# A one-core attention and MLP kernel on Trainium2: five tile pools entered in another order, three small tiles moved

## The chip, the cores and the metric

The kernel runs on one core of a Trainium2 chip. The metric is device time in microseconds (us) of one execution; 1 us is 1000 ns. The core has a matrix engine (PE, with its weight loads shown apart as PEld), a vector engine (DVE), a scalar engine (ACT), a general engine (POOL) and a queue engine that issues most transfers (SP). Operands lie in the on-chip memory SBUF, 128 partitions wide; a tile has the same start address in each partition. Matrix products are written to PSUM.

## The reference

Local attention with a window of 32 and a few global tokens, and then an MLP with gelu, all in float32:

```python
B, H, Sl, D = 8, 8, 512, 64; Sg = 32; window = 32
s_g = scale * q_g @ concat(k_g, k_l).T;  out_g = softmax(s_g) @ concat(v_g, v_l)
s_ll = where(|i - j| <= window, scale * q_l @ k_l.T, -1e9);  s_lg = scale * q_l @ k_g.T
out_l = softmax(concat(s_lg, s_ll)) @ concat(v_g, v_l)
x = concat(out_g, out_l) as (4352, 512)       # 8 * (32 + 512) tokens, 8 heads * 64
h = x @ w_in                                  # 512 -> 2048
g = 0.5 * h * (1 + erf(h / sqrt 2))
out = g @ w_out                               # 2048 -> 512
```

## The kernel before

The tokens are cut into 17 chunks of 256: two halves for each of the 8 batches, and one chunk "g" that gathers the global tokens of all batches. Attention makes a chunk of x in the tile `xs`, head pair by head pair, while the MLP of an earlier chunk runs; a planner with costs and due times, written out at the top of the file, fixes the order of the steps on each engine. PE is shared by both, and its MLP products stand between those of attention.

From the second chunk on, the MLP splits each float32 operand into a high part that float32r holds (`xh`, `gh`, `wh`) and the rest (`xl`, `gl`, `wl`), and adds three products for each one. A product has a stationary operand (`lhsT`), which an LDWEIGHTS loads into the array, and a moving operand (`rhs`), which streams through it:

```python
hi, lo = (w[2 * f][:, c * P:c * P + P] for w in (wh, wl_))          # ml_hc
nc.tensor.matmul(out=h, lhsT=hi, rhs=xh, ...)                       # L709
nc.tensor.matmul(out=h, lhsT=hi, rhs=xl, ...)                       # L710
nc.tensor.matmul(out=h, lhsT=lo, rhs=xh, ...)                       # L711
...
hi, lo = wh[2 * f + 1], wl_[2 * f + 1]                              # ml_o
nc.tensor.matmul(out=acc[t], lhsT=gh[:, f % 2, tsl], rhs=hi, ...)   # L744
nc.tensor.matmul(out=acc[t], lhsT=gl[:, f % 2, tsl], rhs=hi, ...)   # L745
nc.tensor.matmul(out=acc[t], lhsT=gh[:, f % 2, tsl], rhs=lo, ...)   # L746
```

So in the first half of the MLP (lines L709 to L711, tile `h`, 256 columns) the weights are loaded and x streams, and in the second (L744 to L746, tile `acc`, 512 columns) gelu's parts are loaded and the weights stream. For each of 16 values of f a chunk has 12 products of the first kind (three for each of four c) and 6 of the second (three for each of two t). Over 16 chunks that makes 3072 and 1536. The first chunk uses whole float32 products instead (L705, tiles `xf` and `wf`, and L736, tiles `wf` and `gf`).

ACT makes `gf` from `h` (L279), ACT or DVE rounds it to `gh` (L132, L134), POOL subtracts to `gl` (L139). The same helpers make `xh` and `xl` from `xs`. Of attention's products this text uses two: L517 (`o` from `vs`, stationary, and `at`, moving, 256 columns) and L563 (`sg`, the global scores: `gs` is stationary, `k` moving, 288 columns in the first half of a batch and 256 in the second). The two tiles of each `k` part take turns, by whether the head pair is even or odd. L650 (`go` from `agt`, stationary, and `vgs`, moving) serves the global tokens.

SBUF tiles come from pools, and a pool's place follows from the order in which the pools are entered and the sizes of the ones ahead. `cp`, `ap`, `sm`, `gp`, `xp`, `wp` and `wr` are entered in this order; `gp` holds gelu's parts, `xp` holds `xh` and `xl`, `wp` holds `wl` (and `wf`), `wr` holds `wh`, `sm` small columns of the softmax.

Of the kernel before, what the change touches and what calls it, by code (L numbers as in the profile page):

```python
# [8 lines left out]
F32 = mybir.dt.float32  # L9
F32R = mybir.dt.float32r  # L10
BF16 = mybir.dt.bfloat16
# [9 lines left out]
WS, WF = 192, 224  # L21
# [63 lines left out]
def attn_mlp(ctx, tc, q_l, k_l, v_l, q_g, k_g, v_g, w_in, w_out, out):  # L85
# [5 lines left out]
    P = 128  # L91
# [6 lines left out]

    cp = ctx.enter_context(tc.tile_pool(name="cp", bufs=1))
    ap_ = ctx.enter_context(tc.tile_pool(name="ap", bufs=1))  # L100
    sm = ctx.enter_context(tc.tile_pool(name="sm", bufs=4))


    gp = ctx.enter_context(tc.tile_pool(name="gp", bufs=2))
    xp = ctx.enter_context(tc.tile_pool(name="xp", bufs=1))
    ps_s = ctx.enter_context(tc.tile_pool(name="ps_s", bufs=2, space=PSUM))
    ps_t = ctx.enter_context(tc.tile_pool(name="ps_t", bufs=2, space=PSUM))
    ps_h = ctx.enter_context(tc.tile_pool(name="ps_h", bufs=2, space=PSUM))
# [5 lines left out]

    masks = []
    for half in range(2):
        m = cp.tile([P, WF], BF16, name=f"mask{half}")
        nc.gpsimd.memset(m, 0.0)
        for c0, k0, w in (((0, -32, 32), (64, 0, 160)) if half == 0 else ((0, -32, 160), (192, 128, 32))):
            v = m[:, c0:c0 + w]  # L120
            nc.gpsimd.affine_select(out=v, in_=v, pattern=[[-1, w]], base=32 - k0,
                                    channel_multiplier=1, compare_op=ALU.is_ge, fill=-BIG)
            nc.gpsimd.affine_select(out=v, in_=v, pattern=[[1, w]], base=32 + k0,
                                    channel_multiplier=-1, compare_op=ALU.is_ge, fill=-BIG)
        masks.append(m)
# [453 lines left out]
    KG = (0, 160, 288, 416)  # L579

    def gu_min(e, g):
        t = sm.tile([P, 3], F32, name="gsm", tag="gsm", bufs=2)
        st[g, "mn"], st[g, "sum"], st[g, "ri"] = t[:, 0:1], t[:, 1:2], t[:, 2:3]
        mn = st[g, "mn"]
        nc.vector.tensor_reduce(out=mn, in_=sgr[g[1]], axis=AX.X, op=ALU.max)
        nc.vector.tensor_scalar_mul(out=mn, in0=mn, scalar1=-SC)
# [183 lines left out]
    bufs = {"s": 2, "t": 2, "h": 2, "gh": 2, "gl": 2, "sm": 4, "wr": NF}  # L770
# [24 lines left out]
    for n, u in enumerate(units):  # L795
        b, half, p = u
# [209 lines left out]
    def starts(x, k):  # L1006
        t = x["at"][k]
        n = {}
        for kind, y in x["takes"]:
            n[kind] = n.get(kind, 0) + 1  # L1010
        for kind, m in n.items():
            h = sorted((freed.get(y, 1e9) for y in taken.get(kind, [])), reverse=True)
            i = bufs.get(kind, 1) - m
            if i < len(h):
                if h[i] == 1e9:
                    return None
                t = max(t, h[i] + LAT0)
        if k == "a" and x["size"]:
            t = max(t, dma - 1.5)
        return t  # L1020
# [4 lines left out]
    while any(ready.values()):  # L1025
        can = []
        for k in ENG:
            for x in ready[k]:
                t = starts(x, k)
                if t is None:  # L1030
                    continue
                t = max(t, busy[k])
                if k == "p" or k == "v" and x["port"]:
                    t = max(t, port)
# [11 lines left out]
        t, due, _, x, k = best  # L1046
# [86 lines left out]
```

## Time and profile before

| | |
|---|---|
| median of 3 runs | 1050.46 us (1049.86 to 1051.32) |
| the profiled execution | 1050.12 us, of which the span from its first to its last instruction is 1048.3 us |
| PE busy | 1016.1 us, 97% of the span |
| PEld busy | 903.3 us, 86% |
| DVE, ACT, POOL busy | 680.4, 676.9, 380.4 us (65%, 65%, 36%) |
| granted PE clock | 1.00 |

In the groups of instructions a row gives line, engine, operation, tiles (written from read), shape and count, then the busy time in us and the mean duration of one in ns. PE works on several products at a time, so a product's duration is longer than the time from its start to the next one's start. This text calls the latter the pitch; it is read from start times.

### The profile page before, as it was taken

The numbers are of one execution on the slowest core, as the hardware profiler recorded it, in microseconds if no ns is written. First come the engines' busy times: TensorE is split into PE (matmuls) and PEld (weight loads), VectorE is DVE, ScalarE is ACT, GpSimd is POOL, SyncE is SP. The second block draws the span as 40 slices with busy tenths as digits, with TensorE's granted clock in tenths as the row PEclk, the third lists the DMA queues.
The fourth block names the chain that finished last, engine by engine and source line by source line (L and its number), as shares of the span: only waits on it lengthen the run. The fifth ranks groups of instructions, "written<-read, shape, count | busy, mean of one in ns | idle before, by whom it ended". The sixth has DMA issues, their size and how long they took to land.

```text
span 1048.3 us, 21420 instructions
## 1 busy us (share of the span) xinstructions
PE 1016.1 (97%) x7000; PEld 903.3 (86%) x7000; DVE 680.4 (65%) x2089; ACT 676.9 (65%) x1617; POOL 380.4 (36%) x427
## 2 busy tenths in 40 slices
PE   4989999999999999999999999999999999999998
PEld 2756699998988989998999999998999989999897
DVE  2978968667676768677775777577676777561000
ACT  2978886776667766777575666577565766573221
POOL 2111575243332534334342525244333434243121
PEclk9999999999999999999999999999999999999999
DMA  7785332214221233213322332213322332101000
GB/s 186 226 256 201 55 77 45 53 43 81 49 64 30 42 84 65 59 36 60 82 39 56 61 71 59 61 34 76 64 42 51 64 72 59 44 14 56 1 21 21
DMA packets 277983, 72.29 MB, mean 69 GB/s; under 512 B 263152, under 2 KB 271344, under 8 KB 277872
## 3 DMA queue, kind: packets, MB, share of 16 engines
q1 hardware_dynamic: 271792, 68.57, 28.5%
q10 hardware_dynamic: 6080, 2.36, 0.9%
q8 instruction: 55, 0.90, 0.3%
q14 instruction: 56, 0.46, 0.2%
HBM read 61.41 MB, written 9.44 MB: 68 GB/s over the span
## 4 chain that ended last, share of the span: by engine, by line
PE 84%; DMA 4%; ACT 4%; DVE 3%; SPq 3%; issue 1%; POOL 0%; ACTq 0%; DVEq 0%; POOLq 0%
PE h L709 11%; PE h L711 10%; PE h L710 10%; PE acc L744 10%; PE acc L745 10%; PE acc L746 10%; PE o L517 5%; PE s L406 4%; PE t L480 2%; PE acc L736 2%; PE h L705 2%; PE go L650 2%; ACT a_t L279 1%; PE sg L563 1%; DMA wraw<-in_moe_w_in_dram 1%
## 5 line engine op out<-in xcount | busy, mean ns | idle before, releaser
L139 POOL TENSOR_TENSOR gl<-gf,gh 128x512 fp32r<-128x512 f32 x127 | 167.9, 1322 | 406.4 <-ACT gh L132 282.1
L709 PE MATMUL h<-xh,wh 128*128 128x256 f32 x1024 | 299.1, 292 | 1.4 <-ACT gf L279 1.4
L711 PE MATMUL h<-xh,wl 128*128 128x256 f32 x1024 | 289.7, 283 | 0.0
L710 PE MATMUL h<-xl,wh 128*128 128x256 f32 x1024 | 289.3, 283 | 0.0
L744 PE MATMUL acc<-wh,gh 128*128 128x512 f32 x512 | 206.3, 403 | 0.0
L709 PEld LDWEIGHTS h<-xh,wh 128*128 128x128 f32 x1024 | 195.0, 190 | 10.4 <-ACT gf L279 1.8
L745 PE MATMUL acc<-wh,gl 128*128 128x512 f32 x512 | 201.7, 394 | 0.0
L746 PE MATMUL acc<-wl,gh 128*128 128x512 f32 x512 | 200.6, 392 | 0.0
L710 PEld LDWEIGHTS h<-xl,wh 128*128 128x128 f32 x1024 | 195.2, 191 | 5.7 <-issue 0.7
L711 PEld LDWEIGHTS h<-xh,wl 128*128 128x128 f32 x1024 | 195.0, 190 | 0.0
L279 ACT ACTIVATE gf<-h 128x512 f32<-128x512 f32 x136 | 81.1, 597 | 73.2 <-POOL gl L139 37.7
L279 ACT ACTIVATE a_t<-a_t,sm 128x192 f32<-128x192 f32 (+1 forms) x256 | 116.9, 458 | 2.9 <-DVE sm L431 2.0
L746 PEld LDWEIGHTS acc<-wl,gh 128*128 128x128 f32 x512 | 96.4, 188 | 21.6
L425 DVE CUSTOM_DVE_ANT_0 a_t<-s,mask 128x192 f32<-128x192 f32 (+1 forms) x256 | 80.4, 367 | 48.0 <-PE s L406 48.0
L132 ACT ACTIVATE gh<-gf 128x512 fp32r<-128x512 f32 x95 | 60.0, 632 | 77.2 <-PE acc L746 76.1
L744 PEld LDWEIGHTS acc<-wh,gh 128*128 128x128 f32 x512 | 96.9, 189 | 13.0
L745 PEld LDWEIGHTS acc<-wh,gl 128*128 128x128 f32 x512 | 97.0, 189 | 11.3
L500 DVE TENSOR_TENSOR at<-t,at 128x512 fp32r<-128x512 f32 (+1 forms) x112 | 67.7, 618 | 38.7 <-ACT at L132 38.2
L132 ACT ACTIVATE at<-t 128x512 fp32r<-128x512 f32 (+1 forms) x112 | 59.4, 541 | 49.8 <-PE t L481 25.9
L139 POOL TENSOR_TENSOR vs<-vr,vs 128x512 fp32r<-128x512 f32 x56 | 74.8, 1336 | 42.6 <-DVE vs L134 23.9
L279 ACT ACT_TABLE_LOAD x69 | 88.5, 1283 | 1.2
L548 DVE TENSOR_TENSOR xs<-o,xs 64x256 f32<-64x256 f32 x112 | 46.1, 412 | 51.9 <-ACT xs L543 50.6
(132 smaller groups left out, 1730.9 us busy)
## 6 DMA issues: line engine op xcount, KB each, us to landing
wraw<-in_moe_w_out_dram SPq DMA_DIRECT2D x16, 512.0 KB, 7.6
raws<-in_v_l_dram SPq DMA_DIRECT2D x64, 128.0 KB, 2.5
out_dram<-ob SPq DMA_DIRECT2D x32, 256.0 KB, 2.1
raws<-in_k_l_dram SPq DMA_DIRECT2D x224, 36.0 KB, 1.9
vr<-in_v_l_dram SPq DMA_DIRECT2D x113, 64.0 KB, 2.2
wraw<-in_moe_w_in_dram SPq DMA_DIRECT2D x14, 512.0 KB, 7.4
raws<-in_q_l_dram SPq DMA_DIRECT2D x224, 32.0 KB, 1.8
raws<-in_v_g_dram SPq DMA_DIRECT2D x128, 16.0 KB, 1.9
```

The source lines that it names most:

```text
L132: nc.scalar.activation(out=out, in_=in_, func=AF.Copy)
L139: (nc.vector if e == "v" else nc.gpsimd).tensor_sub(**kw)
L279: nc.scalar.activation(func=func, **kw)
L425: nc.vector.tensor_tensor_reduce(out=a_t[:, j, aoff[half][i]:aoff[half][i] + w], in0=s[:, c:c + w], in1=masks[half][i], scale=1.0, scalar= ...
L500: nc.vector.tensor_sub(out=at[:, 1], in0=st.pop((u, "t", j))[:, :n * P].rearrange("p (n q) -> p n q", q=P), in1=at.bitcast(F32)[:, 0])
L517: nc.tensor.matmul(out=o[:, :, qsl], lhsT=l.rearrange("p s e -> p (s e)"), rhs=r, start=(n == 0), stop=(n == 3), skip_group_check=True)
L709: nc.tensor.matmul(out=h, lhsT=hi, rhs=xh, start=(c == 0 and not (key == (0, 0) and f < HQ and f % 2)), stop=False, skip_group_check=True)
L710: nc.tensor.matmul(out=h, lhsT=hi, rhs=xl, start=False, stop=False, skip_group_check=True)
L711: nc.tensor.matmul(out=h, lhsT=lo, rhs=xh, start=False, stop=(c == NCC - 1), skip_group_check=True)
L744: nc.tensor.matmul(out=acc[t], lhsT=gh[:, f % 2, tsl], rhs=hi, start=(f == 0), stop=False)
L745: nc.tensor.matmul(out=acc[t], lhsT=gl[:, f % 2, tsl], rhs=hi, start=False, stop=False)
L746: nc.tensor.matmul(out=acc[t], lhsT=gh[:, f % 2, tsl], rhs=lo, start=False, stop=(f == NF - 1))
```

## The change

`sm` is entered behind `gp` and not ahead of it. One of the two masks moves from `cp` into a new pool `mp`, entered behind `sm`, and the two `gsm` tiles move from `sm` into a new pool `sg`, entered behind `xp`.

```diff
     cp = ctx.enter_context(tc.tile_pool(name="cp", bufs=1))
     ap_ = ctx.enter_context(tc.tile_pool(name="ap", bufs=1))
+    gp = ctx.enter_context(tc.tile_pool(name="gp", bufs=2))
     sm = ctx.enter_context(tc.tile_pool(name="sm", bufs=4))
-    gp = ctx.enter_context(tc.tile_pool(name="gp", bufs=2))
+    mp = ctx.enter_context(tc.tile_pool(name="mp", bufs=1))
     xp = ctx.enter_context(tc.tile_pool(name="xp", bufs=1))
+    sg = ctx.enter_context(tc.tile_pool(name="sg", bufs=2))
...
-        m = cp.tile([P, WF], BF16, name=f"mask{half}")
+        m = (cp if half else mp).tile([P, WF], BF16, name=f"mask{half}")
...
-        t = sm.tile([P, 3], F32, name="gsm", tag="gsm", bufs=2)
+        t = sg.tile([P, 3], F32, name="gsm", tag="gsm")
```

A mask takes 448 bytes of a partition, the four `sm` tiles 4 x 64, the two `gsm` tiles 2 x 32. So all of `cp` behind the mask and all of `ap` start 448 bytes lower, `gp` 448 + 256 + 64 = 768 bytes lower, `xp` 64 bytes lower, and the weights' pools where they were. The order of the instructions on every engine, their shapes and their waits are those of before; only addresses differ. Start addresses of the tiles modulo 512 bytes (each f, c and t step inside a tile is a multiple of 512 bytes):

| tile | before | after |
|---|---|---|
| `xh`, `xl`, `xf` | 448 | 384 |
| `gf`, `gh`, `gl` | 448 | 192 |
| `wh`, `wl`, `wf` | 448 | 448 |
| `agt`, `vgs` (L650) | 448 | 448 |
| `at`, moving in L517 / `vs`, stationary | 128 / 384 | 192 / 448 |
| `gs`, stationary in L563 | 256 | 320 |
| `k` read by L563, 256 columns, even / odd pair | 256 / 0 | 320 / 64 |
| `xs` | 256 | 320 |

## The prediction

> **What bounds the kernel now.** I read the page from the top: busy time and granted clock, then the chain that ended last, then the groups.
>
> ```profile
> PE 1016.1 (97%) x7000; PEld 903.3 (86%) x7000; DVE 680.4 (65%) x2089; ACT 676.9 (65%) x1617; POOL 380.4 (36%) x427
> PEclk9999999999999999999999999999999999999999
> PE 84%; DMA 4%; ACT 4%; DVE 3%; SPq 3%; issue 1%; POOL 0%; ACTq 0%; DVEq 0%; POOLq 0%
> PE h L709 11%; PE h L711 10%; PE h L710 10%; PE acc L744 10%; PE acc L745 10%; PE acc L746 10%; PE o L517 5%; PE s L406 4%; PE t L480 2%; PE acc L736 2%; PE h L705 2%; PE go L650 2%; ACT a_t L279 1%; PE sg L563 1%; DMA wraw<-in_moe_w_in_dram 1%
> L709 PE MATMUL h<-xh,wh 128*128 128x256 f32 x1024 | 299.1, 292 | 1.4 <-ACT gf L279 1.4
> L711 PE MATMUL h<-xh,wl 128*128 128x256 f32 x1024 | 289.7, 283 | 0.0
> L710 PE MATMUL h<-xl,wh 128*128 128x256 f32 x1024 | 289.3, 283 | 0.0
> L744 PE MATMUL acc<-wh,gh 128*128 128x512 f32 x512 | 206.3, 403 | 0.0
> L745 PE MATMUL acc<-wh,gl 128*128 128x512 f32 x512 | 201.7, 394 | 0.0
> L746 PE MATMUL acc<-wl,gh 128*128 128x512 f32 x512 | 200.6, 392 | 0.0
> ```
>
> PE is busy all through at the full granted clock, and the six MLP lines alone hold 11+10+10+10+10+10 = 61% of the chain, 639 us. The other engines are busy two thirds of the time or less. So the time is a count of products times their pitch, and a nanosecond on each MLP product is about 4.6 us on PE (3072 + 1536 of them). How long a product holds PE, and how its successor's load runs beside it, is in the order of time, first near the end, where attention no longer stands between, then in the middle:
>
> ```profile
> 1000.25 0.28 PE L709 MATMUL h<-xh,wh 128*128 128x256 f32 x1
> 1001.69 0.40 PE L744 MATMUL acc<-wh,gh 128*128 128x512 f32 x1
> 1003.08 0.28 PE L709 MATMUL h<-xh,wh 128*128 128x256 f32 x1
> ```
>
> ```profile
> 600.05 0.28 PE L710 MATMUL h<-xl,wh 128*128 128x256 f32 x1
> 600.06 0.19 PEld L711 LDWEIGHTS h<-xh,wl 128*128 128x128 f32 x1
> ```
>
> Between the first two starts lie 12 products of 256 columns: 1.44 us / 12 = 120 ns each. Between the second and the third lie 6 of 512 columns: 1.39 / 6 = 232 ns each. Together 3072 x 0.120 + 1536 x 0.232 = 725 us of pitch, of which the chain's 639 us are 88%. The other pair shows the load for the next product (L711) starting 0.01 us after the running product (L710): one reads its moving tile while the other reads the next stationary tile. What the change alters is the distance of these two addresses.
>
> **The change, part by part.** I write the distance as start of the running product's moving tile minus start of the tile that is loaded beside it, modulo 512 bytes, from the table of addresses.
> - L709 to L711 (3072): x moves, weights are loaded. 448 - 448 = 0 before; 384 - 448 = -64, that is 448, after.
> - L744 to L746 (1536): weights move, gelu's parts are loaded. 0 before; 448 - 192 = 256 after. (From L711 into L744 it is 192 after, from L746 into L709 it stays 0.)
> - L517 (256), L563 and L650 keep their distances.
>
> Does the distance matter at all? The trace has one line that runs at two of them: L563 with 256 columns has distance 0 for even head pairs and 256 for odd ones (it loads `gs` for its second product while the first streams). The view of one line's instructions gives the duration in ns, here for one first product of an even pair, then of an odd pair, 0.6 us later:
>
> ```profile
> L563 PE MATMUL sg<-k,gs x1: 288/288/288, 653.9 to 653.9; 128*128 128x256 f32 x1
> L563 PE MATMUL sg<-k,gs x1: 282/282/282, 654.5 to 654.5; 128*128 128x256 f32 x1
> ```
>
> Six nanoseconds less at 256 than at 0. The lines with hundreds of products say the same more weakly (lowest/median/highest, loads and products; the count behind the last shape is not of all):
>
> ```profile
> L710 PEld LDWEIGHTS h<-xl,wh x1024: 187/192/193, 124.4 to 1038.0; 128*128 128x128 f32 x171
> L710 PE MATMUL h<-xl,wh x1024: 273/283/288, 124.5 to 1038.1; 128*128 128x256 f32 x171
> L711 PE MATMUL h<-xh,wl x1024: 278/283/288, 124.6 to 1038.2; 128*128 128x256 f32 x171
> L517 PEld LDWEIGHTS o<-at,vs x448: 186/188/193, 140.0 to 940.6; 128*128 128x128 f32 x150
> L517 PE MATMUL o<-at,vs x448: 273/281/386, 140.1 to 940.7; 128*128 128x256 f32 x150
> L650 PEld LDWEIGHTS go<-vgs,agt x128: 186/192/193, 84.1 to 960.3; 128*128 128x128 f32 x128
> L650 PE MATMUL go<-vgs,agt x128: 274/283/468, 84.1 to 960.5; 128*128 128x256 f32 x128
> ```
>
> L710, L711 and L650, all at distance 0, have loads of 192 ns and products of 283; L517, at 256, has 188 and 281. So I take it that the two reads get in each other's way where the tiles start at the same place modulo 512.
>
> First term, L709 to L711. Distance 448 is seen only where L563 with 288 columns is followed by L709, at odd pairs of a first half; two such, in a quicker and a slower spell:
>
> ```profile
> L563 PE MATMUL sg<-k,gs x2: 293/294/294, 833.5 to 833.6; 128*128 128x288 f32 x2
> L563 PE MATMUL sg<-k,gs x2: 293/295/297, 863.1 to 863.3; 128*128 128x288 f32 x2
> L563 PE MATMUL sg<-k,gs x1: 302/302/302, 626.3 to 626.3; 128*128 128x288 f32 x1
> ```
>
> The second products took 293 and 297 ns. Thirty-two columns more are worth 13 ns by the step from 256 to 512 columns ((232 - 120) / 256 = 0.44 ns a column, 14; a little less without the stall). So 256 columns at distance 448 would take 280 to 284, mean 282, against 283: 1 ns less; L517's 281 says 2. I take 1.5 ns: 3072 x 1.5 = 4.6 us. The bounds: the best is 278, the lowest of L711, which is 5 ns, 15.4 us; the worst is the last row above, a 288-column product at distance 384 (302 - 13 = 289), which is 6 ns more, 18.4 us.
>
> Second term, L744 to L746:
>
> ```profile
> L745 PE MATMUL acc<-wh,gl x512: 386/394/399, 149.4 to 1043.4; 128*128 128x512 f32 x171
> L746 PE MATMUL acc<-wl,gh x512: 387/390/402, 149.6 to 1043.6; 128*128 128x512 f32 x171
> L744 PE MATMUL acc<-wh,gh x512: 386/396/498, 149.1 to 1043.1; 128*128 128x512 f32 x171
> ```
>
> Mean of the medians: (396 + 394 + 390) / 3 = 393.3 ns. L563's step from 0 to 256 takes 6 off. But L746 is at distance 0 too and has 390, close to the lowest of all (386), so it can't lose 6. I take 5, which leaves 388: 1536 x 5 = 7.7 us. The bounds: 7 ns (the lowest, 386) is 10.8 us; 0 if L746's low value means that something other than the distance sets L744 and L745.
>
> The rest. The mask that moves is read by L425 on DVE, `sm` and `gsm` by short instructions of DVE and ACT. They cost no instruction more, and the distance of DVE's and ACT's own operands is not seen to matter: ACT's copies of 256 columns take 413 and 415 ns at source and target 256 and 192 bytes apart (`q` and `xh`, below). DVE, ACT and POOL have a third of the span to spare; were L425's 80.4 us a tenth longer, 8 us would be spread over 64 units, behind the PE work of the chunk before. The weights' transfers land where they did.
>
> ```profile
> L132 ACT ACTIVATE xh<-xs 128x256 fp32r<-128x256 f32 x62 | 25.4, 415 | 16.8 <-PE h L711 15.9 <-DVE xs L549 0.4 <-PE h L705 0.2
> L132 ACT ACTIVATE q<-qt 128x256 fp32r<-128x256 f32 x31 | 12.8, 413 | 8.2 <-DVE qt L332 7.7
> L425 DVE CUSTOM_DVE_ANT_0 a_t<-s,mask 128x192 f32<-128x192 f32 (+1 forms) x256 | 80.4, 367 | 48.0 <-PE s L406 48.0
> ```
>
> Sum: 4.6 + 7.7 = 12.3 us of PE time, 88% of it on the chain: 10.8 us. The profiled execution's 1050.12 us becomes 1039.3; the median lies 0.3 us above that execution, which I leave inside the rounding: 1039.5 us.
>
> **The rivals.**
>
> *The distance does not matter* (the change doesn't do what it says). For it: the first chunk's products stream at distance 0 too and show no stall. In the chain:
>
> ```profile
> 95.10 1.72 PE acc L736 x4
> 96.82 1.73 PE h L705 x8
> ```
>
> That is 430 ns for 512 columns and 216 for 256, so exactly two to one, with nothing fixed beside it. And L746 beats L745 at the same distance. Against it: whole float32 products take near twice as long a column as float32r ones, so they read more slowly, and L563's 6 ns is one line at two distances. The time would be 1050.5, chance 0.12. The Trainium skill has this as a rule: "SBUF — State Buffer", section "SBUF: two separate sides", lets contention among engines come from the port pair of DVE and GpSimd alone, and "TensorE: Matmul & The Clock Gate", section "Step-by-step: what each phase is for", says that loading the next weights doesn't steal read bandwidth from the running matmul. By that rule the sum is 0; L563's two rows speak against it, L736's and L705's agree.
>
> *-64 is a bad place for x* (slower). At distance 384 a product took 302 ns where two others of its size took 293; if 448 behaves like that in the long runs of L709 to L711, they lose 6 ns: 18.4 us, less 7.7 from the second half, times 0.88: 9.4 us more, 1059.9. It decides from 7.7 / 3.07 = 2.5 ns a product on. Against it: the two products at 448 itself. Chance 0.13, half of it between 1052.6 and 1056.
>
> *All stalls go.* Durations fall to the lowest seen, 273 (L710) to 278 and 386: up to 8 ns on the first kind (24.6 us) and 7 on the second (10.8 us), times 0.88: 31 us, 1019. For it: the lowest values are seen at distance 0 already, so the array can do it. Against it: L517 at 256 still has a median of 281. Chance 0.10.
>
> *PE gains, the end does not.* `gf` waits for POOL's `gl` for 37.7 us in all now; with shorter products the chain gelu, `gh`, `gl` has less cover. If half of the 10.8 us came back as waits, 1045. Chance 0.13; PE stands idle for 32 us of 1048 in all, so most of that work is done early today.
>
> ```profile
> ACT gf L279 <- POOL gl L139: 37.7, 30, 3.6
> ```
>
> **How the numbers follow.** My forecast, 1034 to 1044, has 0.52; the half-hidden gain 0.13, all stalls 0.10, no effect 0.12, slower 0.13. The range leaves out most of the full gain and the farther half of the slower case: 1025 to 1055. Within 0.2% (2.1 us, about what a measurement of this kernel can tell from no change) lies the no-effect case; faster sums to 0.75, slower is 0.13.
>
> **What would show it.** In the changed kernel's profile L710's and L711's mean should be 281 to 282 with loads of 188, L744 to L746 near 388 at the median, 12 products of the first kind in 1.42 us and 6 of the second in 1.36; L517, L563 and L650 unchanged, PE's busy time down by some 11 us with its share still 97%. If loads stay at 192 and products at 283, the distance was not the cause; if L709 to L711 rise to 286 or more, -64 is a bad place; if they fall to 278 or less, the stalls were larger than one neighbour shows. PE's idle growing by 5 us would be the hidden gain.

## The result and the profile after

The changed kernel takes 1042.93 us (median of 5 runs, 1041.08 to 1045.66) against 1050.51: a ratio of 0.9926, interval 0.9905 to 0.9946. That is 0.74% less, where 1.05% was forecast, inside the range. Its profiled execution is the slowest of the five, 1045.66 us with a span of 1043.8, so the trace shows less of the gain than the median does. The page's rows (two lines are new in the file, so L709 is now L711 and so on):

```profile
PE 1006.6 (96%) x7000; PEld 894.8 (86%) x7000; DVE 684.9 (66%) x2089; ACT 677.0 (65%) x1617; POOL 379.7 (36%) x427
PE 75%; ACT 7%; SPq 6%; DMA 5%; DVE 4%; issue 2%; POOL 1%; ACTq 0%; DVEq 0%; POOLq 0%
L711 PE MATMUL h<-xh,wh 128*128 128x256 f32 x1024 | 296.6, 290 | 1.4 <-ACT gf L281 1.4
L712 PE MATMUL h<-xl,wh 128*128 128x256 f32 x1024 | 286.1, 279 | 0.0
L713 PE MATMUL h<-xh,wl 128*128 128x256 f32 x1024 | 285.6, 279 | 0.0
L746 PE MATMUL acc<-wh,gh 128*128 128x512 f32 x512 | 204.9, 400 | 0.0
L748 PE MATMUL acc<-wl,gh 128*128 128x512 f32 x512 | 200.4, 391 | 0.0
L747 PE MATMUL acc<-wh,gl 128*128 128x512 f32 x512 | 200.2, 391 | 0.0
```

PE's busy time fell by 9.5 us. The mean duration of L712 and L713 went from 283 to 279 ns, that of the second half's three lines by 3, 3 and 1 ns. The view of single lines (lowest/median/highest) and three starts from the order of time, near the end:

```profile
L712 PEld LDWEIGHTS h<-xl,wh x1024: 187/188/192, 127.8 to 1033.5; 128*128 128x128 f32 x171
L712 PE MATMUL h<-xl,wh x1024: 276/281/288, 127.9 to 1033.7; 128*128 128x256 f32 x171
L746 PE MATMUL acc<-wh,gh x512: 387/389/499, 152.2 to 1038.6; 128*128 128x512 f32 x171
L747 PE MATMUL acc<-wh,gl x512: 387/389/398, 152.6 to 1038.9; 128*128 128x512 f32 x171
```

```profile
996.42 0.28 PE L711 MATMUL h<-xh,wh 128*128 128x256 f32 x1
997.83 0.39 PE L746 MATMUL acc<-wh,gh 128*128 128x512 f32 x1
999.19 0.28 PE L711 MATMUL h<-xh,wh 128*128 128x256 f32 x1
```

Loads fell from a median of 192 to 188 ns. Twelve products of the first half now take 1.41 us and six of the second 1.36, against 1.44 and 1.39. These rows are not the mean of the execution: elsewhere the first half runs quicker still. Six products in the middle of the execution took 0.68 us, 113 ns each:

```profile
448.06 0.28 PE L711 MATMUL h<-xh,wh 128*128 128x256 f32 x1
448.74 0.28 PE L711 MATMUL h<-xh,wh 128*128 128x256 f32 x1
```

Of the changed kernel's 138 groups of twelve that ran without a wait, 65 have a mean pitch between 113 and 116 ns (from the first start to the twelfth) and 73 one between 117 and 118, with none in between. Before, all 139 such groups lie between 117.9 and 120.3. So one distance gives more than one pitch; what picks it was not tested.

Where the time stands: from the first to the last start of L710 (now L712) it was 1038.1 - 124.5 = 913.6 us and is 1033.7 - 127.9 = 905.8, so 7.8 us less. But that stretch begins 3.4 us later in this execution, in the part where the weights arrive. The windows from 40 to 80 us, before and after (time; then busy time and count of PE, PEld, DVE, ACT, POOL; granted clock, DMA share, GB/s):

```profile
40.00:80.00 40.00, 34.45 (x185) 24.59 (x183) 30.87 (x92) 31.37 (x75) 6.21 (x10) 1.00 0.76 230
```

```profile
40.00:80.00 40.00, 33.51 (x175) 24.96 (x174) 29.04 (x88) 28.48 (x71) 5.43 (x9) 0.96 0.72 216
```

Transfers ran at 216 instead of 230 GB/s there, and PE had a lower granted clock for a while. The windows behind the start, before and after:

```profile
124.40:1043.60 919.20, 913.15 (x6472) 831.34 (x6471) 589.07 (x1838) 588.51 (x1411) 351.42 (x377) 1.00 0.25 52
```

```profile
127.80:1039.00 911.20, 902.86 (x6472) 822.13 (x6471) 593.30 (x1838) 588.27 (x1411) 350.99 (x377) 1.00 0.25 52
```

There PE's idle time grew from 6.1 to 8.3 us; in the whole span it grew from 32.2 to 37.2. In the profiles of the twelve kernels below this first start lies anywhere from 122.7 to 127.5 us, whatever the places of the tiles, so I take it as scatter of the executions and read the change from the stretch behind it and from the medians.

### The profile page after: what moved, and what is told of

The parts are those of the page before. It is cut to its first block, busy times and chain, and to the rows that moved or that the text cites. A ratio compares the mean times of both kernels' runs of the same rounds, so it can differ in the third digit from the quotient of the medians.

```text
span 1043.8 us, 21420 instructions
## 1 busy us (share of the span) xinstructions
PE 1006.6 (96%) x7000; PEld 894.8 (86%) x7000; DVE 684.9 (66%) x2089; ACT 677.0 (65%) x1617; POOL 379.7 (36%) x427
## 4 chain that ended last, share of the span: by engine, by line
PE 75%; ACT 7%; SPq 6%; DMA 5%; DVE 4%; issue 2%; POOL 1%; ACTq 0%; DVEq 0%; POOLq 0%
PE h L711 10%; PE acc L746 9%; PE h L712 9%; PE h L713 9%; PE acc L748 9%; PE acc L747 9%; PE o L519 5%; PE s L408 4%; PE acc L738 2%; PE t L482 2%; ACT a_t L281 2%; PE h L707 2%; PE go L652 2%; ACT L281 1%; DMA raws<-in_q_l_dram 1%
## 5 line engine op out<-in xcount | busy, mean ns | idle before, releaser
L711 PE MATMUL h<-xh,wh 128*128 128x256 f32 x1024 | 296.6, 290 | 1.4 <-ACT gf L281 1.4
L712 PE MATMUL h<-xl,wh 128*128 128x256 f32 x1024 | 286.1, 279 | 0.0
L713 PE MATMUL h<-xh,wl 128*128 128x256 f32 x1024 | 285.6, 279 | 0.0
L746 PE MATMUL acc<-wh,gh 128*128 128x512 f32 x512 | 204.9, 400 | 0.0
L711 PEld LDWEIGHTS h<-xh,wh 128*128 128x128 f32 x1024 | 192.7, 188 | 10.2 <-ACT gf L281 1.8
L712 PEld LDWEIGHTS h<-xl,wh 128*128 128x128 f32 x1024 | 193.0, 188 | 5.7 <-issue 0.7
L713 PEld LDWEIGHTS h<-xh,wl 128*128 128x128 f32 x1024 | 193.9, 189 | 0.0
L746 PEld LDWEIGHTS acc<-wh,gh 128*128 128x128 f32 x512 | 96.3, 188 | 12.2
```

The source lines that it names most:

```text
L711: nc.tensor.matmul(out=h, lhsT=hi, rhs=xh, start=(c == 0 and not (key == (0, 0) and f < HQ and f % 2)), stop=False, skip_group_check=True)
L712: nc.tensor.matmul(out=h, lhsT=hi, rhs=xl, start=False, stop=False, skip_group_check=True)
L713: nc.tensor.matmul(out=h, lhsT=lo, rhs=xh, start=False, stop=(c == NCC - 1), skip_group_check=True)
```

## The experiments

All twelve kernels have the instructions, order and waits of the kernel before; only pools and small tiles are placed otherwise. In each diff below A is what lies ahead of `gp`, B what lies between `gp` and `xp`, C what lies behind `xp` and ahead of the weights; gsm, sm, mask0, mask1 and sgr0 or sgr1 stand for the pools that hold these tiles. A distance is that of the streaming from the loaded tile, as in the prediction, but modulo 256, for a reason that the runs gave; -64 is 192. A pitch is the mean start-to-start time of the trace over the products that waited for nothing (those with less than 137 ns to the next start with 256 columns, and 243 with 512; 4 to 5% are left out), for L709 to L711 and for L744 to L746.

| kernel | x | gelu | pitch, first half | pitch, second half | ratio to before (interval) |
|---|---|---|---|---|---|
| before | 0 | 0 | 119.2 | 230.9 | |
| after | -64 | 0 | 116.3 | 229.1 | 0.9926 (0.9905 to 0.9946) |
| x_only | -64 | 0 | 116.3 | 229.1 | 0.9927 (0.9908 to 0.9947) |
| x_mod256 | -64 | 0 | 116.4 | 229.0 | 0.9935 (0.9922 to 0.9948) |
| moved_w | -64 | 0 | 116.3 | 229.2 | 0.9924 (0.9908 to 0.9940) |
| dx192_dg192 | -64 | 192 | 115.9 | 232.8 | 0.9943 (0.9928 to 0.9958) |
| dx32_dg32 | 32 | 32 | 117.4 | 232.0 | 0.9961 (0.9946 to 0.9976) |
| dx64_dg128 | 64 | 128 | 117.5 | 232.3 | 0.9981 (0.9969 to 0.9993) |
| x_behind32 | -32 | 0 | 118.3 | 231.0 | 0.9997 (0.9986 to 1.0008) |
| x_behind96 | -96 | 0 | 118.5 | 230.1 | 0.9986 (0.9975 to 0.9997) |
| dx128_dg64 | 128 | 64 | 118.9 | 231.2 | 1.0009 (0.9997 to 1.0021) |
| g_only | 0 | 0 | 119.2 | 230.9 | 1.0006 (0.9994 to 1.0018) |
| both256 | 0 | 0 | 119.3 | 231.1 | 1.0025 (1.0013 to 1.0038) |
| cp_shift | 0 | 0 | 119.3 | 231.1 | 1.0023 (1.0010 to 1.0037) |

### x alone, gelu's parts alone, the attention tiles alone, and both at 256

```diff
 before:   A = sm (with gsm)     B =          C =
+x_only:   A = sm                B = mask0    C = gsm      # x 384, gelu 448 modulo 512
+g_only:   A = gsm               B = sm       C =          # x 448, gelu 192
+cp_shift: A = sm gsm mask0      B =          C =          # x 448, gelu 448, attention +64
+both256:  A = gsm mask0         B =          C = sm       # x 192, gelu 192
```

> Only the distance of x from the weights is changed (448 modulo 512, as in the changed kernel); gelu's parts stay at distance 0 from the weights. Both theories expect the first half's products (L709 to L711) at a mean of 279 ns with loads of 188, as in the changed kernel: 3072 products at 2.7 ns less, 8 us on PE. Theory A (acc products gain from their own distance): L744 and L745 stay at 394 to 396 at the median; time 1043 to 1044. Theory B (acc products gain because they follow less congested loads): L744 and L745 fall to 389 to 391 here too; time 1041 to 1042. Rival (the change acts by another way, the attention tiles' places): 1050.

> Only the distance of gelu's parts from the weights is changed (256 modulo 512); x and attention's tiles lie as before. L709 to L711 stay at 283 with loads of 191. Theory A: L744 and L745 fall from 394-396 to 389-391 at the median, 2 ns less on the mean, time 1048 to 1049. Theory B: they stay above 393, time 1050 to 1051.

The groups of x_only and then of g_only (one line fewer in its file, so L709 and L744 there are L710 and L745 of before):

```profile
L710 PE MATMUL h<-xl,wh 128*128 128x256 f32 x1024 | 287.1, 280 | 0.0
L744 PE MATMUL acc<-wh,gh 128*128 128x512 f32 x512 | 204.9, 400 | 0.0
L745 PE MATMUL acc<-wh,gl 128*128 128x512 f32 x512 | 200.2, 391 | 0.0
```

```profile
L709 PE MATMUL h<-xl,wh 128*128 128x256 f32 x1024 | 289.4, 283 | 0.0
L743 PE MATMUL acc<-wh,gh 128*128 128x512 f32 x512 | 206.1, 403 | 0.0
L744 PE MATMUL acc<-wh,gl 128*128 128x512 f32 x512 | 201.5, 394 | 0.0
```

x_only has the whole effect, in the second half's lines too (400 and 391, as in the changed kernel), though gelu's parts did not move against the weights. g_only has none of it: 403 and 394 as before, ratio 1.0006. So theory B holds: the second half's products gain because of what the first half does ahead of them, and moving gelu's parts is worth nothing here. By place among the six of a group, the pitch fell from before to x_only by 3.2, 3.7, 0.6, 2.2, 2.0 and 0.2 ns, so the gain reaches the fourth and fifth product behind x too. One thing is not separated: the first load of `gh` runs beside the last product of x, and with gelu's parts at 0 its distance moves together with x.

> One mask moves behind the attention pools, so that all attention tiles start 64 bytes higher modulo 512, as in the changed kernel, while x, gelu's parts and the weights stay at one place (distance 0). The distance theory: L709 to L711 at 283, L744 to L746 at 390 to 396, time 1050.5, no change. Rival (places of the attention tiles, or of the mask, bring the gain): 1043.

> x and gelu's parts lie at the same place, both 256 bytes from the weights modulo 512. If what counts is the distance of the streaming tile from the loaded tile, x and gelu may share a place: L709 to L711 at 279 to 281 (L517 has 281 to 282 at 256), loads of 188, L744 and L745 at 389 to 391, time 1041 to 1045. If x and gelu's parts must differ from each other, 1050.

```profile
L710 PE MATMUL h<-xl,wh 128*128 128x256 f32 x1024 | 289.1, 282 | 0.0
L711 PE MATMUL h<-xh,wl 128*128 128x256 f32 x1024 | 289.4, 283 | 0.0
L745 PE MATMUL acc<-wh,gl 128*128 128x512 f32 x512 | 201.8, 394 | 0.0
```

These three rows of both256 read the same, digit for digit, in cp_shift. The attention tiles' move, which the changed kernel makes too, brings nothing; both kernels are even 0.2% slower than before, with L517 at 283 ns at the median instead of 281 (448 products, 0.9 us of that), though the distance of L517's own operands is the same. And a distance of 256 is as bad as 0. My expectation for both256 failed: either x and gelu's parts must differ, or the distance counts modulo 256.

### A scan of distances

```diff
+dx128_dg64:  A = sm gsm      B = mask0         C = sgr0               # x 320, gelu 384
+dx64_dg128:  A = sm gsm      B = mask1         C = mask0              # x   0, gelu  64
+dx192_dg192: A = sm          B = sgr0          C = gsm                # x 384, gelu 256
+dx32_dg32:   A = sm gsm[1]   B = sgr0 mask1    C = mask0 gsm[0]       # x 480, gelu 416
+x_mod256:    A =             B = mask0         C = sm gsm             # x 128, gelu 192
+x_behind32:  A = sm          B = mask0 gsm[1]  C = gsm[0]             # x 416, gelu 448
+x_behind96:  A = sm          B = sgr1 gsm[1]   C = mask0 sgr0 gsm[0]  # x 352, gelu 192
```

> x streams 128 bytes away from the loaded weights (modulo 256), the weights stream 64 away from gelu's parts. If what counts is the distance modulo 256 and every distance but 0 is good: L710 and L711 at a mean of 279 to 280 with loads of 188, time 1043. If it is modulo 128: 283 with loads of 192, time 1051. If gelu's distance counts in the same way once it isn't 0 modulo 256 (so far 0 and 256 were tried, which would be one place): L744 to L746 below the 389 of the changed kernel at the median, 386 to 387, another 3 us.

> x streams 64 bytes ahead of the loaded weights (before the edit 0, in the changed kernel 64 behind), the weights stream 128 from gelu's parts. Modulo 256 or 128 and every distance but 0 good: L710 and L711 at 279 to 280, time 1043. If the sign matters (the stream runs into the load's place or away from it): 281 or more. L744 to L746 at 386 to 387 if gelu's distance counts modulo 256; 389 if it does not, or counts modulo 128.

> x as in the changed kernel (448, which is 192 modulo 256), the weights 192 from gelu's parts instead of 256, which is 0 modulo 256. L710 and L711 at 279 to 280 as in the changed kernel. L744 to L746: 389 if gelu's distance does not count, 386 to 387 if it counts modulo 256 or 128; time 1042.9 or 1040.

> Both distances 32 bytes modulo 256. If the places that collide are narrower than 32 bytes: L710 and L711 at 279 to 280 with loads of 188, time 1043 or less. If they are 64 bytes wide: 283 with loads of 192, time 1051; between the two, 281.

The groups of dx128_dg64, and of dx192_dg192 (its L745 and L746):

```profile
L711 PE MATMUL h<-xl,wh 128*128 128x256 f32 x1024 | 289.4, 283 | 0.0
L712 PE MATMUL h<-xh,wl 128*128 128x256 f32 x1024 | 289.9, 283 | 0.0
```

```profile
L746 PE MATMUL acc<-wl,gh 128*128 128x512 f32 x512 | 202.6, 396 | 0.0
L745 PE MATMUL acc<-wh,gl 128*128 128x512 f32 x512 | 202.3, 395 | 0.0
```

Not every distance but 0 is good: at 128 the first half is as slow as at 0. A period of 128 would give that too, but then 64 and -64 would be one place, and they have 117.5 and 116.3 ns. For gelu's parts, 192 is worse than 0: dx192_dg192 has x as in the changed kernel and 232.8 against 229.1 ns, which is 1536 x 3.7 = 5.7 us on PE. Less of it shows in the time: its median is 1045.88 us, and the interval of its ratio overlaps with that of the changed kernel. At 32, 64 and 128 gelu's parts moved together with x, so their 231.2 to 232.3 ns, against 229.0 to 231.1 in all kernels with gelu's parts at 0, do not single out gelu's distance. My expectation that gelu's parts would gain once they left 0 modulo 256 was wrong in sign.

> x starts 320 bytes below the weights modulo 512, which is 64 below modulo 256; the weights stream 256 from gelu's parts, which is 0 modulo 256. If only the distance modulo 256 counts: as the changed kernel, L710 and L711 at 279 to 280 with loads of 188, pitch 116.3 ns, L744 to L746 at 389, time 1043. If it is modulo 512: unknown for x at 192, but L517 and L563 there had 116 to 117 ns, about the same for x; gelu's parts at 256 have been tried and are as at 0. So a time near 1051 would say that 512 counts and that 192 is bad.

> x 32 bytes behind the weights, gelu's parts at 0. With x 32 ahead the pitch of L709 to L711 was 117.4 ns, 64 ahead 117.5, 64 behind 116.3, 0 and 128 both 119. If behind is better than ahead at every size: 116 to 117 and a time of 1043 to 1045. If 64 behind is the one good place: 118 or more, 1048. L744 to L746 at 389 (gelu at 0).

> x 96 bytes behind the weights, gelu's parts at 0 modulo 256. If behind is better and the best lies between 64 and 128: 115 to 116 ns, 1040 to 1042. If the pitch rises from 64 to 128 evenly: 117.6 ns, 1046. L744 to L746 at 389 to 390.

x_mod256 puts x at -320, that is -64 modulo 256, and has the changed kernel's pitches and time. So of the two readings of both256, modulo 256 holds. The other two fell short: 32 and 96 behind lose most of the gain (118.3, 118.5), so "behind is better" is wrong as well. Among the seven distances modulo 256 that were tried, -64 is the best place for x, 32 and 64 ahead have about 60% of its gain in the first half, and the curve is not smooth.

### The distance or x's own place

In all these the weights stood still, so x's own place could have been the cause. The last kernel moves the weights.

```diff
+moved_w: A = sm    B = mask0    C = sgr0 mask1    behind the weights and vgs, agt: gsm
+         # x 320, gelu 384, weights 384 modulo 512
```

> Distances as in the quick kernels (x 64 behind the weights, gelu's parts at 0 modulo 256), but all three lie at other places: the weights and gelu's parts 64 bytes lower than in any run so far (128 modulo 256), x where it was in the run with x 128 behind (64 modulo 256), which gained nothing. If the distance counts: L709 to L711 at a pitch of 116.3 ns, L710 and L711 at 279 to 280, L744 to L746 at 389, time 1043 to 1044. If x's own place counts: as that run, 118.9 ns, 282 to 283, time 1052.

```profile
L712 PE MATMUL h<-xl,wh 128*128 128x256 f32 x1024 | 286.7, 280 | 0.0
L713 PE MATMUL h<-xh,wl 128*128 128x256 f32 x1024 | 286.3, 280 | 0.0
L747 PE MATMUL acc<-wh,gl 128*128 128x512 f32 x512 | 200.2, 391 | 0.0
```

x at 320 was slow with the weights at 448 (dx128_dg64) and is quick with the weights at 384. The distance counts, not the place. Its ratio, 0.9924, is that of the changed kernel; none of the twelve beats that beyond its interval.

The same kernel bears on the row on which the prediction stood. `k` and `gs` of L563 lie here where they lay before, modulo 512 (256 or 0, and 256). Before, the first product of an even pair took 288 ns and of an odd pair 282. Here, an even and an odd pair in one window (L565 in this file):

```profile
L565 PE MATMUL sg<-k,gs x4: 278/278/283, 649.1 to 649.8; 128*128 128x256 f32 x4
```

The 288 is gone: the first product takes 278 ns in the even pair and 279 in the odd one, with nothing moved between this line's own operands. So the row did not show the distance of `k` from `gs`. What changed is what stands around it: the pitch of x's products ahead, the distance of x from `gs`, which is loaded beside the last of them, and that of `k` from the weights loaded next. The runs do not separate these. It is not simply a slow pitch handed on from one product to the next, since the product just ahead of the 288 had 117 ns to its next start and the one ahead of the 282 had 121.

## Why the prediction was right or wrong, point by point

- *The bound, and the share on the chain.* The bound was right: PE's pitch made the gain. The share was too high. By pitch PE saved 3072 x 2.9 + 1536 x 1.8 = 11.7 us, against the 12.3 of the sum. In the stretch behind the start 7.8 us of it came through, 67% and not 88%. PE's share of the chain, 84% before, is 75% in the changed kernel's profile and 81% in those of x_only and moved_w, so what the prediction took from the kernel before did not hold.
- *Gain hidden by waits* (the fourth rival) is part of that: the products of the six lines that did wait, by the same limits, were 191 with 52.1 us from start to next start and became 194 with 55.5, which is 3.4 of the 3.9 us that did not come through. The sign that the prediction named for it, 5 us more of idle time on PE, came, though only 2.3 of the 5 stand behind the start.
- *First term* (x, 1.5 ns, 4.6 us): sign right, size half. Measured 2.9 ns, 8.9 us. It was read from single L563 products at 448; the long runs at one distance do better, and the load's 192 going to 188 was the better sign.
- *Second term* (gelu's parts, 5 ns, 7.7 us): measured 1.8 ns, 2.8 us, and its cause was wrong. None of it comes from gelu's parts; 256 is the same place as 0, as g_only shows, and the gain is a consequence of x's (x_only). The warning was in the prediction's own rows: L746, at the same distance, had 390 and not 396. The two errors offset each other. That the total came out near is luck.
- *L563 as proof that the distance matters:* the step that failed. Modulo 256 both pairs lie at 0, and the difference between them is gone in moved_w, where their own distances are those of before. L517, the second support, fails in the same way: its 256 is 0 modulo 256 as well, and in cp_shift it has 283 ns at that distance and not 281. The conclusion was right for x all the same.
- *The distance does not matter* (rival): refuted by x_only against g_only and cp_shift. The Trainium skill, in "TensorE: Matmul & The Clock Gate", section "Step-by-step: what each phase is for", has it that the load of the next weights takes nothing from the running product's reads. For these float32r streams the trace disagrees: moving x by 64 bytes against the loaded weights is worth 2.9 ns a product, and the loads themselves went from 192 to 188 ns. How the two reads meet, no run here shows.
- *-64 is a bad place:* refuted; it is the best of those tried. *All stalls go:* no; L712 has a mean of 279 ns, where the lowest seen before was 273.
- *The signs named:* loads of 188 came, 12 and 6 products in 1.41 and 1.36 us (1.42 and 1.36 named); L712 went to 279, lower than the 281 to 282 named; PE's busy time fell by 9.5 us, where some 11 were named.

Not settled: why -64 is good and 128 is not, why the second half is better at 0 than at 192, and why one distance has more than one pitch. The runs give the curve and the period, not the mechanism.

## What to carry to other kernels

Where PE is the bound and its products stream float32r with a load beside each, the distance between the streaming and the loaded tile is worth trying, modulo 256 bytes: moving a few small tiles gave 0.7% here with no instruction changed. Scan it on each kind of product by itself, since the two halves of this MLP did best at different distances (-64 and 0), and judge a candidate by long runs of one line. Two short products that differ may differ by what stands around them, so before a row is used as evidence for a cause, look at its neighbours.

## What the runs showed of the hardware that was not expected

- The pitch of float32r products depends on the distance of the streaming from the loaded tile: first half 116.3 ns at -64, 117.4 to 117.5 at 32 and 64, 118.3 to 118.5 at -32 and -96, 118.9 to 119.3 at 128, 0 and 256.
- The period is at most 256 bytes and not 128: 256 acts as 0 (119.3 and 119.2 ns), -320 as -64 (116.4 and 116.3), while 64 and -64 (117.5 and 116.3) differ.
- The pitch also depends on what runs around a product, with its own operands at the same distance: second half 230.9 to 229.1 ns by x alone, L563's first product from 288 to 278 ns.
- One distance can have more than one pitch: at -64, groups of twelve ran at 113 to 116 ns or at 117 to 118.
